# One softmax per pair of tiles in a fused attention and MLP kernel, and a bias joined by accumulating DMAs

## The chip, the cores and the metric

The kernel runs on one core of a Trainium2 chip. The metric is device time in microseconds (us), as the median of several executions. A core has a matrix engine (TensorE, "PE" in the profile, with its weight loads as "PEld"), a vector engine (VectorE, "DVE"), a scalar engine for activations (ScalarE, "ACT"), GpSimd ("POOL"), and SyncE ("SP"). In this kernel SP does nothing but issue DMAs. The engines run side by side and wait for one another by semaphores. In the traces of this case, SP's DMAs are issued in the order in which the program was written: in the changed kernel a load whose buffer VectorE had finished reading at 219.0 us was issued at 226.19 us, behind the two transposes written ahead of it (SP's lines are shown below).

An instruction that waits in SP's queue holds up every DMA written behind it.

## The reference, cut to what matters

```python
# S = 2048 positions, D = 576, H = 32 heads, W = 8 keys per position, spaced 2 apart
h  = x + softmax_w(q . k[s - 2w]) @ v[s - 2w] @ wo        # from layernorm(x) @ wqkv
h2 = h + gelu(layernorm(h) @ w1 + b1) @ w2 + b2           # F = 4608
```

Each position attends to itself and to the seven positions 2, 4, ..., 14 before it. The positions are cut into 16 tiles of 128, even tiles first, then odd ones, and eight *groups* (pairs of tiles) go through the rest of the kernel one after the other.

## The kernel before: the parts that matter

For every group, TensorE does three blocks: MLP1 (four "visits" of PSUM banks), the wo product of the next group, and MLP2. Beside it, VectorE and ScalarE prepare later groups: attention of the tiles e and f two groups ahead, and LayerNorm of the tiles c and d one group ahead.

Attention needs no matrix engine here. QK multiplies q by eight K rows and adds them up in a tree; PV does the same with V. Both use the one scratch tile `prod`. K and V of the eight tiles of one parity lie in a ring. After a tile has used a ring slot, the slot is refilled from DRAM with the rows shifted by one (`halo`), for the next tile of that parity:

```python
def halo(j, t):                       # t = 1: K, t = 2: V
    if j >= 2:
        ring = (None, k_ring, v_ring)[t]
        nc.sync.dma_start(out=ring[j % 2][:, j // 2, :], in_=kv_dram[j, 0:P, t - 1, :])

def pv_sum(j):
    att_pv_sum(j)                     # one 2.56 us multiply, three adds, on VectorE
    halo(j, 2)
```

So QK of f must wait until the K halo load issued after QK of e has landed, and PV of f waits for the V halo load issued after PV of e. LayerNorm's result crosses DRAM to be transposed:

```python
def ln2_send(j):                      # ScalarE, then two DMAs on SP's queue: hn -> td
    ...
    hn[j] = dma_out(y[:])
def ln2_in(j):                        # a transposing DMA on SP's queue: td -> hnT
    nc.sync.dma_start_transpose(out=hnT_slot(j), in_=hn.pop(j)[:])
def add_b2(j):                        # VectorE
    nc.vector.tensor_tensor(out=x_all[:, j, :], in0=h_of.pop(j)[:], in1=b2_bc[:], op=ALU.add)
def marker(mm_ins):                   # end of a half's visit, on GpSimd's queue
    nop = nc.gpsimd.nop().ins
    ...
```

The schedule of a group k, with c, d the next group and e, f the one after (cut):

```python
m1[0].append(c_(pv_t, d))                               # in MLP1: PV left over from the last group
m1[3] = [c_(att_qk, e)] + [c_(w2_sums, ...)]            # in MLP1, last visit: QK of e
ia[0] = [c_(exps, e), c_(wo_visit, (c, "B"), (d, "C")), c_(ln2_pair, c, d, e)]
ia[2] = [c_(pv_sum, e), c_(dma_tr_o, e)]                # in MLP2, first tile: PV of e
ib[0] = [c_(finish_out, g[0])]                          # evict the first tile of MLP2
ib[2] = [c_(att_qk, f)] + ([c_(halos, 7)] if k == 1 else [])   # in MLP2, second tile: QK of f
ib[32] = [c_(exps, f)]
```

In the trace of before, QK of e and QK of f start some 20 us apart (118.90 and 138.36 us in the second group), and PV of e and PV of f 16 us apart (132.53 and 148.65 us), with other work between.

## Time and profile before

| | before |
|---|---|
| time, median of runs | 371.8 us |
| TensorE / VectorE / ScalarE / GpSimd busy | 363.2 / 299.3 / 239.1 / 25.2 us |
| one group (MLP1 + wo + MLP2) | 17.79 + 2.21 + 17.75, period 37.74 us |
| TensorE waits over 0.3 us after 94 us | none |

First the busy times on the page of the kernel before (microseconds, share of the span, instructions):

```profile
PE 363.2 (98%) x4944; PEld 299.4 (81%) x4944; DVE 299.3 (81%) x452; ACT 239.1 (65%) x519; POOL 25.2 (7%) x35
```

A busy share does not yet say who sets the time. The chain of waits does. This is a part of it for the kernel before (start, length, what):

```profile
93.92 14.81 PE po L505 x120
108.72 17.79 PE pm L209 x324
126.52 2.21 PE pw L209 x36
128.72 17.75 PE po L505 x144
146.47 17.79 PE pm L209 x324
...
350.77 15.55 PE po L576 x126
366.35 0.46 DVE o_sb L599
```

Each line begins where the last one ended: from 93.9 us to the end the chain is TensorE and nothing else. VectorE is 81% busy and on the chain nowhere in that stretch, apart from the last eviction.

SP's queue in the kernel before, in the second group (start, length of issue; x2 is two in a row): hn of two tiles is written, transposed back, then the V halo load.

```profile
137.44 0.34 SPq L185 DMA_DIRECT2D td<-hn  x1
137.83 0.42 SPq L186 DMA_DIRECT2D td<-hn  x1
138.53 0.33 SPq L185 DMA_DIRECT2D td<-hn  x1
138.91 0.42 SPq L186 DMA_DIRECT2D td<-hn  x1
139.47 2.52 SPq L433 DMA_TRANSPOSE hnT<-td  x2
142.09 0.53 SPq L314 DMA_DIRECT2D kv_ring<-kv_dram  x1
```

And the DMA issues of the kernel before (count, KB each, median us from issue to landing):

```profile
td<-hn SPq DMA_DIRECT2D x14, 144.0 KB, 1.8
td<-hn SPq DMA_DIRECT2D x14, 16.0 KB, 1.6
hnT<-td SPq DMA_TRANSPOSE x14, 2.9
```

An hn write lands in 1.8 us, a transpose in 2.9 us.

### The profile page before, as it was taken

The numbers are of one execution on the slowest core, as the hardware profiler recorded it, in microseconds if no ns is written. First come the engines' busy times: TensorE is split into PE (matmuls) and PEld (weight loads), VectorE is DVE, ScalarE is ACT, GpSimd is POOL, SyncE is SP. The second block draws the span as 40 slices with busy tenths as digits, with TensorE's granted clock in tenths as the row PEclk, the third lists the DMA queues.
The fourth block names the chain that finished last, engine by engine and source line by source line (L and its number), as shares of the span: only waits on it lengthen the run. The fifth ranks groups of instructions, "written<-read, shape, count | busy, mean of one in ns | idle before, by whom it ended". The sixth has DMA issues, their size and how long they took to land.

```text
span 369.8 us, 11478 instructions
## 1 busy us (share of the span) xinstructions
PE 363.2 (98%) x4944; PEld 299.4 (81%) x4944; DVE 299.3 (81%) x452; ACT 239.1 (65%) x519; POOL 25.2 (7%) x35
## 2 busy tenths in 40 slices
PE   7999999999999999999999999999999999999996
PEld 4789877888788877887788778877887788778874
DVE  6899999999999798979897989889898986532332
ACT  2688756797738793679366936693669456735630
POOL 2322004000300010001000100000000000000000
PEclk9999999999999999999999999999999999999999
DMA  8979798956445104710431043104320411030000
GB/s 242 318 198 282 190 204 235 331 178 76 141 107 166 35 15 111 275 35 2 110 97 37 2 106 102 37 2 105 86 52 3 105 52 39 0 89 18 4 0 32
DMA packets 57265, 38.96 MB, mean 105 GB/s; under 512 B 31344, under 2 KB 55536, under 8 KB 57216
## 3 DMA queue, kind: packets, MB, share of 16 engines
q1 hardware_dynamic: 57056, 38.18, 38.6%
q8 instruction: 38, 0.62, 0.7%
q10 hardware_dynamic: 160, 0.07, 0.1%
q14 instruction: 11, 0.09, 0.1%
HBM read 19.92 MB, written 12.42 MB: 87 GB/s over the span
## 4 chain that ended last, share of the span: by engine, by line
PE 84%; DVE 11%; ACT 2%; POOL 1%; issue 1%; POOLq 0%; DVEq 0%
PE pm L209 37%; PE po L505 29%; PE po L576 8%; PE pw L209 5%; PE pq L209 4%; DVE ln_stats L145 2%; DVE prod L323 2%; DVE prod L362 1%; DVE prod L317 1%; PE busy L661 1%; DVE prod L366 1%; POOL ln_rstd L156 1%; ACT hT L490 1%; DVE ln_mv L146 1%; ACT L463 0%
## 5 line engine op out<-in xcount | busy, mean ns | idle before, releaser
L209 PE MATMUL pm<-hnT,w_sb 64*128 64x256 bf16 x2304 | 143.0, 269 | 0.5 <-ACT hT L490 0.5
L490 ACT ACTIVATE hT<-pm,b_sb 128x256 bf16<-128x256 f32 (+1 forms) x288 | 108.5, 498 | 48.4 <-PE pm L209 48.4
L209 PEld LDWEIGHTS <-w_sb 64*128 64x128 bf16 x2304 | 112.5, 94 | 15.0 <-issue 2.3
L505 PEld LDWEIGHTS <-hT 128*128 128x128 bf16 x864 | 84.0, 98 | 22.6 <-issue 1.7
L505 PE MATMUL po<-w2a_sb,hT 128*128 128x288 bf16 x672 | 84.5, 286 | 0.0
L209 PE MATMUL pq<-wq_sb,xnT 64*128 64x288 bf16 x768 | 54.0, 283 | 0.4 <-ACT xnT L255 0.2
L209 PEld LDWEIGHTS <-xnT 64*128 64x128 bf16 x864 | 44.1, 94 | 9.1 <-issue 0.4
L323 DVE TENSOR_TENSOR prod<-prod 128x2304 bf16<-128x2304 bf16 (+1 forms) x64 | 44.2, 691 | 2.1
L362 DVE TENSOR_TENSOR prod<-kv_ring,a 128x4608 bf16<-128x4608 bf16 x16 | 40.9, 2558 | 0.6
L317 DVE TENSOR_TENSOR prod<-kv_ring,q_all 128x4608 bf16<-128x4608 bf16 x16 | 40.8, 2552 | 0.2
L209 PE MATMUL pm<-hnT,w1h_sb 64*128 64x256 bf16 x288 | 39.4, 269 | 0.0
L366 DVE TENSOR_TENSOR prod<-prod 128x2304 bf16<-128x2304 bf16 (+1 forms) x32 | 33.9, 1058 | 1.1
L345 ACT ACTIVATE logits<-logits 128x256 f32<-128x256 f32 x16 | 6.7, 417 | 38.1 <-DVE logits L334 38.1
L423 POOL TENSOR_TENSOR ln_rstd<-ln_var,mhalf 128x1 f32<-128x1 f32 x14 | 11.3, 810 | 249.8 <-ACT ln_var L422 249.6
L505 PE MATMUL po<-w2b_sb,hT 128*128 128x288 bf16 x192 | 25.5, 286 | 0.0
L294 ACT CAST kv_ring<-pq 128x576 bf16<-128x576 f32 x32 | 19.4, 641 | 8.4 <-PE pq L209 8.4
L407 DVE TENSOR_TENSOR h<-pw,x_all 128x576 f32<-128x576 f32 x16 | 11.4, 751 | 14.0 <-PE pw L209 14.0
L209 PE MATMUL pw<-wo_sb,oT 64*128 64x288 bf16 x256 | 19.5, 283 | 0.2
L463 ACT ACT_TABLE_LOAD x14 | 18.0, 1283 | 0.2
L552 DVE TENSOR_TENSOR prod<-hT 128x512 f16<-128x512 f16 (+1 forms) x8 | 3.6, 455 | 17.6 <-ACT hT L490 17.6
L209 PEld LDWEIGHTS <-oT 64*128 64x128 bf16 x288 | 13.9, 94 | 4.3 <-POOLq L219 0.8
L345 ACT ACT_TABLE_LOAD x13 | 16.7, 1283 | 0.2
(98 smaller groups left out, 340.4 us busy)
## 6 DMA issues: line engine op xcount, KB each, us to landing
w_sb<-in_B_w_dram SPq DMA_DIRECT2D x6, 768.0 KB, 6.0
kv_ring<-kv_dram SPq DMA_DIRECT2D x28, 144.0 KB, 2.8
w2a_sb<-in_B_w_dram SPq DMA_DIRECT2D x4, 1008.0 KB, 6.5
kv_dram<-kv_ring SPq DMA_DIRECT2D x13, 288.0 KB, 3.5
out_dram<-o_sb SPq DMA_DIRECT2D x15, 144.0 KB, 2.9
td<-q_all SPq DMA_DIRECT2D x14, 144.0 KB, 2.4
td<-hn SPq DMA_DIRECT2D x14, 144.0 KB, 1.8
wq_sb<-in_A_wqkv_dram SPq DMA_DIRECT2D x3, 576.0 KB, 5.9
```

Source lines behind the costliest of these rows:

```text
L209: last = nc.tensor.matmul(duo["g"][r ^ swap][i], lhsT=lhsT, rhs=rhs, start=(swap == 0 and i == 0 and kt == 0), stop=(swap == 1 and kt == K ...
L294: pace[0] = nc.scalar.copy(out=dst.rearrange("p (d g h) -> p g d h", g=2, h=H // 2), in_=ps[:, :, 0:HALF].rearrange("p g (h d) -> p g d h" ...
L317: nc.vector.tensor_tensor(out=prod[:], in0=k_ring[j % 2], in1=q_all[:, j, :].unsqueeze(1) .to_broadcast([P, W, D]), op=ALU.mult)
L323: nc.vector.tensor_tensor(out=prod[:, :, o * H:o * H + n], in0=prod[:, :, a * H:a * H + n], in1=prod[:, :, c * H:c * H + n], op=ALU.add)
L345: nc.scalar.activation(out=logits[:], in_=logits[:], func=ACT.Exp, scale=SCALE)
L362: nc.vector.tensor_tensor(out=prod[:].rearrange("p w (d h) -> p w d h", h=H), in0=v_ring[j % 2].rearrange("p w (d h) -> p w d h", h=H), in ...
L366: nc.vector.tensor_tensor(out=prod[:, 0:n, :], in0=prod[:, 0:n, :], in1=prod[:, n:2 * n, :], op=ALU.add)
L407: nc.vector.tensor_tensor(out=h[:].rearrange("p (g c) -> p g c", g=2), in0=pw[:, :, 0:HALF], in1=x_all[:, j, :].rearrange("p (g c) -> p g ...
L463: nc.scalar.activation(out=warm[:], in_=mhalf[:], func=ACT.Gelu_apprx_tanh)
L490: pace[0] = nc.scalar.activation(out=hT[us[i // GF]][:, GF * r + i % GF, 0:N], in_=ps[:, r, i * N:(i + 1) * N], func=ACT.Gelu_apprx_tanh, ...
L505: nc.tensor.matmul(banks[half], lhsT=hT[f // (2 * GF)][:, f % (2 * GF), i * P:(i + 1) * P], rhs=w2_rows(f)[:, half * HALF:(half + 1) * HAL ...
L576: nc.tensor.matmul(bank, lhsT=l, rhs=r, start=(start and m == 0), stop=(m == NM - 1), skip_group_check=True)
```

## The change

Its intent is to relieve VectorE and ScalarE. One max, subtract, exp, sum, reciprocal and product per *pair* of tiles replaces one per tile, which also saves switching of ScalarE's tables between Exp and Gelu (28 table loads in the trace of before). For that, both QK stand together in MLP1 and both PV together in MLP2. The b2 adds leave VectorE: SP's queue copies b2 into `x_all`, and GpSimd's queue adds h to it with an accumulating DMA. The diff, cut to its core:

```diff
+    def put_b2(j):
+        nc.sync.dma_start(out=x_all[:, j, :], in_=b2_bc[:])
+
+    def accumulate_h(j):
+        nc.gpsimd.dma_start(out=x_all[:, j, :], in_=h_of.pop(j)[:], accum_op=ALU.add)
 ...
-        def ln2_pair(c, d, e, b2=True):
+        def ln2_pair(c, d):
             for j in (c, d):
                 ln2_h(j)
                 ln2_act(j)
             for j in (c, d):
-                if b2:
-                    add_b2(j)
+                put_b2(j)
+            for j in (c, d):
+                accumulate_h(j)
                 ln2_send(j)
             for j in (c, d):
                 ln2_in(j)
-            if e is not None:
-                att_den(e)
 ...
+                if k == 1:                       # changeover from the old order to the new
+                    m1[0].append(c_(pv_t, d))
+                    m1[1] = [c_(att_qk_a, e), c_(halo, e, 1), c_(att_qk_b, e, 0)]
+                    m1[3] = [c_(att_qk_a, f), c_(halo, f, 1)]
+                    ia[0] = wo + [c_(att_qk_b, f, 1), c_(att_max, (e, f)), c_(exps, e, f), c_(att_den, e, f)]
+                    ia[2] = [c_(pv_sum, e), c_(dma_tr_o, e), c_(halos, 4)]
+                elif e is not None:
+                    m1[1] = [c_(att_qk_pair, e, f)]
+                    m1[3] = [c_(w2_sums, *m) for m in T_SUMS.get(k, ())]
+                    ia[0] = [c_(exps, e, f)] + wo + [c_(att_den, e, f)]
+                    ia[2] = [c_(pv_sum, e), c_(dma_tr_o, e)]
 ...
-                    ib[2] = [c_(att_qk, f)] + ([c_(halos, 7)] if k == 1 else [])
-                    ib[32] = [c_(exps, f)]
+                    ib[2] = [c_(pv_sum, f), c_(dma_tr_o, f)] + ([c_(halos, 3)] if k == 1 else [])
```

The softmax tiles become four fixed tiles of double width, and the first LayerNorm's statistics move to another pool to make room.

More of the change, by code (lines that the diff above doesn't have):

```diff
@@ L82 @@
     prod = wpool.tile([P, W, D], BF16, name="prod")
+    logits = wpool.tile([P, 2, W, H], F32, name="logits")
+    probs = wpool.tile([P, 2, W, H], BF16, name="probs")
+    peak = wpool.tile([P, 2, H], F32, name="peak")
+    den = wpool.tile([P, 2, H], F32, name="den")
     qp_cm = tc.tile_pool(name="qkvw", bufs=1)
@@ L140, in ln_stats @@
         n = len(srcs)
-        stats = sb.tile([P, n, 2, nc.vector.BN_STATS_DIM], F32, tag=f"{tag}_stats", name=f"{tag}_stats", bufs=bufs)
-        mv = sb.tile([P, n, nc.vector.BN_AGGR_DIM], F32, tag=f"{tag}_mv", name=f"{tag}_mv", bufs=bufs)
+        pool = qp if tag.startswith("ln1") else sb
+        stats = pool.tile([P, n, 2, nc.vector.BN_STATS_DIM], F32, tag=f"{tag}_stats", name=f"{tag}_stats", bufs=bufs)
+        mv = pool.tile([P, n, nc.vector.BN_AGGR_DIM], F32, tag=f"{tag}_mv", name=f"{tag}_mv", bufs=bufs)
         for i, src in enumerate(srcs):
@@ L306, in tr_b1, with sides @@
         nc.scalar.copy(out=b1_sb[:], in_=pt)
-    e_of = {}
+    side = {}
+    def sides(js):
+        i = side[js[0]]
+        return slice(i, i + len(js))
     def halo(j, t):
@@ L324, in att_qk_add, with att_qk_b, att_max, att_qk_rest @@
                                     in1=prod[:, :, c * H:c * H + n], op=ALU.add)
-    def att_qk_b(j, skip=0):
+    def att_qk_b(j, i, skip=0):
+        side[j] = i
         att_qk_add(j, ((0, 0, 9), (0, 0, 4), (0, 0, 2), (0, 0, 1))[skip:])
-        logits = sb.tile([P, W, H], F32, tag="logits", name="logits", bufs=2)
-        nc.vector.tensor_tensor(out=logits[:], in0=prod[:, :, 0:H], in1=prod[:, :, 8 * H:9 * H], op=ALU.add)
+        nc.vector.tensor_tensor(out=logits[:, i], in0=prod[:, :, 0:H], in1=prod[:, :, 8 * H:9 * H], op=ALU.add)
         if j // 2 + 1 < W:
-            nc.vector.memset(logits[0:1, j // 2 + 1:W, :], -1e9)
-        mx = sb.tile([P, H], F32, tag="mx", name="mx")
-        nc.vector.tensor_reduce(out=mx[:], in_=logits[:].rearrange("p w h -> p h w"), axis=AX.X, op=ALU.max)
-        nc.vector.tensor_tensor(out=logits[:], in0=logits[:], in1=mx[:].unsqueeze(1).to_broadcast([P, W, H]),
-                                op=ALU.subtract)
-        e_of[j] = logits
-    def att_qk(j):
+            nc.vector.memset(logits[0:1, i, j // 2 + 1:W, :], -1e9)
+    def att_max(js):
+        n, sl = len(js), sides(js)
+        nc.vector.tensor_reduce(out=peak[:, sl], in_=logits[:, sl].rearrange("p i w h -> p i h w"), axis=AX.X, op=ALU.max)
+        nc.vector.tensor_tensor(out=logits[:, sl], in0=logits[:, sl],
+                                in1=peak[:, sl].unsqueeze(2).to_broadcast([P, n, W, H]), op=ALU.subtract)
+    def att_qk_rest(j, i, skip=0):
+        att_qk_b(j, i, skip)
+        att_max([j])
+    def att_qk(j, i):
         att_qk_a(j)
         halo(j, 1)
-        att_qk_b(j)
-    def att_exp(j):
-        logits = e_of[j]
-        nc.scalar.activation(out=logits[:], in_=logits[:], func=ACT.Exp, scale=SCALE)
+        att_qk_rest(j, i)
+    def att_qk_pair(e, f):
+        for i, j in enumerate((e, f)):
+            att_qk_a(j)
+            halo(j, 1)
+            att_qk_b(j, i)
+        att_max([e, f])
+    def att_exp(*js):
+        sl = sides(js)
+        nc.scalar.activation(out=logits[:, sl], in_=logits[:, sl], func=ACT.Exp, scale=SCALE)
     def att_pv(j):
@@ L349, in att_pv, with att_den @@
         att_pv_sum(j)
-    def att_den(j):
-        e = e_of.pop(j)
-        den = sb.tile([P, H], F32, tag="den", name="den")
-        nc.vector.tensor_reduce(out=den[:], in_=e[:].rearrange("p w h -> p h w"), axis=AX.X, op=ALU.add)
-        nc.vector.reciprocal(out=den[:], in_=den[:])
-        a = sb.tile([P, W, H], BF16, tag="a", name="a")
-        nc.vector.tensor_tensor(out=a[:], in0=e[:], in1=den[:].unsqueeze(1).to_broadcast([P, W, H]), op=ALU.mult)
-        e_of[j] = a
+    def att_den(*js):
+        n, sl = len(js), sides(js)
+        nc.vector.tensor_reduce(out=den[:, sl], in_=logits[:, sl].rearrange("p i w h -> p i h w"), axis=AX.X, op=ALU.add)
+        nc.vector.reciprocal(out=den[:, sl], in_=den[:, sl])
+        nc.vector.tensor_tensor(out=probs[:, sl], in0=logits[:, sl],
+                                in1=den[:, sl].unsqueeze(2).to_broadcast([P, n, W, H]), op=ALU.mult)
     def att_pv_sum(j):
-        a = e_of.pop(j)
+        a = probs[:, side.pop(j)]
         nc.vector.tensor_tensor(out=prod[:].rearrange("p w (d h) -> p w d h", h=H),
                                 in0=v_ring[j % 2].rearrange("p w (d h) -> p w d h", h=H),
-                                in1=a[:].unsqueeze(2).to_broadcast([P, W, Dh, H]), op=ALU.mult)
+                                in1=a.unsqueeze(2).to_broadcast([P, W, Dh, H]), op=ALU.mult)
         for n in (4, 2):
@@ L747 @@
             6: [c_(ln1_rstd, 10), c_(ln1_act, 8, 2), c_(halo, A[0], 1)],
-            7: [c_(att_qk_b, A[0]), c_(ln1_bias, 10), c_(ln1_act, 8, 3), c_(in_x, 0), c_(out_x, 1)],
-            8: [c_(att_qk_a, A[1]), c_(att_qk_b, A[1]), c_(ln1_act, 9, 0)],
+            7: [c_(att_qk_rest, A[0], 0), c_(ln1_bias, 10), c_(ln1_act, 8, 3), c_(in_x, 0), c_(out_x, 1)],
+            8: [c_(att_qk_a, A[1]), c_(att_qk_rest, A[1], 1), c_(ln1_act, 9, 0)],
             9: [c_(halo, A[1], 1), c_(in_x, 1)],
@@ L760 @@
             19: [c_(ln2, A[1])],
-            20: [c_(ln2_rstd, A[1]), c_(add_b2, A[1]), c_(ln2_bias, A[1]), c_(att_qk_b, A[2], 1)],
+            20: [c_(ln2_rstd, A[1]), c_(add_b2, A[1]), c_(ln2_bias, A[1]), c_(att_qk_rest, A[2], 0, 1)],
         }
@@ L817, in halos, with exps @@
                 store_halo(pending_halo.pop(0))
-        def exps(j):
-            att_exp(j)
+        def exps(*js):
+            att_exp(*js)
             gelu_table()
@@ L836 @@
             if k == 0:
-                m1[0] += [c_(halos, 1), c_(att_qk_a, d), c_(att_qk_b, d), c_(halo, d, 1)]
+                m1[0] += [c_(halos, 1), c_(att_qk_a, d), c_(att_qk_rest, d, 1), c_(halo, d, 1)]
                 mid[0] = [c_(exps, d)]
-                m1[1] = [c_(pv_t, c), c_(pv_t, d), c_(load_w2, 4), c_(att_qk, e)]
+                m1[1] = [c_(pv_t, c), c_(pv_t, d), c_(load_w2, 4), c_(att_qk, e, 0)]
                 ia[0] = [c_(wo_visit, (c, "B"))]
-                ia[12] = [c_(exps, e), c_(wo_visit, (d, "A")), c_(ln2_pair, c, d, e, False), c_(pv_sum, e), c_(dma_tr_o, e), c_(halos, 2)]
+                ia[12] = [c_(exps, e), c_(wo_visit, (d, "A")), c_(ln2_pair, c, d), c_(att_den, e), c_(pv_sum, e),
+                          c_(dma_tr_o, e), c_(halos, 2)]
@@ L842 @@
                 ib[0] = [c_(finish_out, g[0])]
-                ib[4] = [c_(att_qk, f)]
+                ib[4] = [c_(att_qk, f, 1)]
                 ib[32] = [c_(exps, f)]
             elif c is not None:
-                m1[0].append(c_(pv_t, d))
+                wo = [c_(wo_visit, (c, "B"), (d, "C")), c_(ln2_pair, c, d)]
                 if k == 1:
-                    m1[0] += [c_(add_b2, j) for j in g]
-                if e is not None:
-                    m1[3] = m1.get(3, []) + [c_(att_qk, e)] + [c_(w2_sums, *m) for m in T_SUMS.get(k, ())]
-                    ia[0] = [c_(exps, e)]
@@ L852 @@
-                ia[0] = ia.get(0, []) + [c_(wo_visit, (c, "B"), (d, "C")), c_(ln2_pair, c, d, e)]
+                    m1[0].append(c_(pv_t, d))
[8 more added lines that the diff above has]
+                    ia[2] = [c_(pv_sum, e), c_(dma_tr_o, e)]
+                else:
+                    ia[0] = wo
@@ L853 @@
                 ib[0] = [c_(finish_out, g[0])]
                 if e is not None:
-                    ia[2] = [c_(pv_sum, e), c_(dma_tr_o, e)]
-                    ib[2] = [c_(att_qk, f)] + ([c_(halos, 7)] if k == 1 else [])
-                    ib[32] = [c_(exps, f)]
+                    ib[2] = [c_(pv_sum, f), c_(dma_tr_o, f)] + ([c_(halos, 3)] if k == 1 else [])
             if g in fast:
```

## The prediction

> **What bounds the kernel now.** TensorE. The page gives it 98% busy at full granted clock. The chain of waits, in order of time, is TensorE alone from 93.9 us to the last eviction at 366.4: per group of two tiles 17.79 us MLP1, 2.21 us wo, 17.75 us MLP2, with no gap (period 37.74). The change touches no matmul. VectorE (81%) and ScalarE (65%) are off the chain there. The gaps before 79 us lie in code the change leaves alone. So the change can remove nothing from the chain; it can only add waits.
>
> **What it removes, per full group.** VectorE: two b2 adds (0.75 each) and some fixed cost of the small softmax operations (max 0.59, subtract 0.42, sum 0.59, reciprocal 0.35, product 0.42 become one double-width operation per pair): about 2 us of about 34. ScalarE: one pair of table loads (2 x 1.28) and an exp: about 2.8 us. I value both at zero.
>
> **What it adds.** Two b2 copies on SP's queue and two accumulating GpSimd-queue DMAs per group, and 4 us or more of PV moved from MLP1 into MLP2. GpSimd's queue also carries the no-ops that mark ends of a visit; accumulations issue just after wo, about 10 us before the next marker, so I expect no wait there. The Trainium skill, "DMA: Bandwidth & Descriptors", section "SWDGE vs HWDGE vs iDMA", says accumulation is tied to GpSimd's software descriptor path; the before trace has no such DMA to compare. Two cost estimates from the durations above: pair max 1.1, pair softmax finish 2.5 us.
>
> **Where I expect new waits: in the changeover groups, k=1 and k=2; later groups fit (about 32 us of VectorE in 37.7).**
> 1. k=1 does a leftover PV, a QK, half a QK, then after wo the other half, exp, and both PVs. VectorE estimate: exp ready 138, softmax 140.7, PV e 145.9, eviction 146.6, PV f 151.9, and only then the second tile's eviction, 152.6. The second group of MLP1's second visit wants that PSUM pair at 151.5: about 1 us of TensorE wait (0 to 2.5).
> 2. SP's queue is in order: transpose of PV f waits for its write (2 to 3.3 us as in before), three K/V stores follow (0.7 each), so the first odd halo load issues only near 161 and lands near 164 (2.8 us median). VectorE's second QK of k=2 waits for it; the pair's max, the weight sums and then h after wo come near 175 instead of 166.0. LayerNorm and transposes take about 12 us more (before: h 166.0, last transpose issued 179.7), so hnT lands near 187 where MLP1 wants it at 185.4: about 2 us (0 to 4.5).
> 3. At the end of k=0, hnT lands about 0.3 us before it is needed; accumulation traffic could cost up to 1 us.
>
> Sum about 2.7 us.
>
> **Prediction: 374.5 us; range 371.6 to 378.5.** Faster by over 2%: 0.01; within 2%: 0.92; slower by over 2%: 0.07.
>
> **What would show it.** Right: TensorE matmul busy total unchanged; chain still TensorE, but with a VectorE eviction of MLP2's second tile near 150 us and a DMA or ScalarE piece near 185 us; VectorE idle waiting for a halo load near 160 us; ScalarE with about five table-load pairs fewer; steady groups still 37.74 us apart. Wrong: chain unbroken (time equal), or waits of TensorE on GpSimd's queue at every MLP1.
>
> **What would make it wrong.** Descriptor work for the accumulations slow enough under VectorE's traffic to block markers (several us per group, over 2% slower); accumulations delaying the hnT transposes in every group; the halo stores draining faster than I estimate (then no loss); a hidden cost of before that VectorE's relief cures, which I see no sign of.

## The result, and the profile after

The first four runs of the changed kernel gave a median of 388.56 us (383.81 to 394.67), against 371.79 (371.74 to 371.90) of the kernel before. That is 4% slower and outside the predicted range. Two of the four runs were slow: they were over 1.5% above the fastest of their own kernel; this kernel scatters by itself. Ratios here are the mean time of one kernel's fast runs over the mean of the other's fast runs of the same rounds, so not quite the ratio of the medians: 1.037 (95% interval 1.032 to 1.042) from those runs, and 1.044 (1.037 to 1.051) from a later repetition.

The busy times of the changed kernel:

```profile
PE 365.5 (95%) x4944; PEld 310.3 (80%) x4944; DVE 285.6 (74%) x413; ACT 224.8 (58%) x499; POOL 40.0 (10%) x49
```

The intent was met: VectorE does 13.7 us less and ScalarE 14.3 us less. None of it became time. The span went from 369.8 to 385.6 us. The waits list of the changed kernel (who waited for whom, us in total, times, longest) shows new entries for TensorE and VectorE:

```profile
PE pm L214 <- DVE o_sb L657: 6.8, 4, 1.9
PE pm L214 <- DMA hnT<-td: 4.6, 2, 2.3
PE pm L214 <- DVE logits L345: 1.7, 1, 1.7
DVE prod L381 <- DMA kv_ring<-kv_dram: 25.3, 4, 6.4
DVE prod L326 <- DMA kv_ring<-kv_dram: 10.0, 6, 4.0
DVE rest L624 <- DMA x_all<-h: 4.4, 1, 4.4
```

The first three are the loss: 13.1 us of TensorE waiting in MLP1 blocks. (The third, at 110.31 us, is put down to VectorE's `logits`, which merely came last by the profile; b2_only below has the same wait at the same place, put down to hnT.) Adding 1.7 us of half clock (below) gives 14.8 of the 15.8 us. The fourth and fifth lines are where they come from. L381 is the PV multiply, L326 the QK multiply. VectorE waits four times for about 6.3 us until a V halo load has landed, before PV of f. The chain of waits of the changed kernel, from one such wait to the next (many short pieces left out), is a closed loop that hardly touches TensorE:

```profile
186.75 2.40 DMA kv_ring<-kv_dram
189.25 2.57 DVE prod L381
...
194.40 0.75 DVE o_sb L657
195.15 2.48 DVE prod L326
...
199.73 2.36 DMA kv_ring<-kv_dram
202.11 2.57 DVE prod L326
...
212.85 1.34 DVE h L426 x2
...
221.07 3.77 DMA td<-hn
224.89 1.20 SPq L452
226.19 2.46 DMA kv_ring<-kv_dram
228.75 2.57 DVE prod L381
```

Read it as follows. The V halo load lands, so PV of f runs, then the eviction of MLP2's second tile (`o_sb`, for which TensorE waits), then QK of e, a K halo load, QK of f, the weight sums, and h of the next group. LayerNorm, the hn write and the transposes follow, and only then comes the next V halo load, because it stands behind all of that *in SP's queue*. From PV of f to PV of f this takes 228.75 - 189.25 = 39.5 us, and the following turns take about as long. TensorE needs 37.74 us per group, so the loop now sets the pace, with a wait of 1.5 to 1.9 us each time: these waits end at 195.20, 234.70, 274.14 and 313.95 us, which is 39.5, 39.4 and 39.8 us apart. The load needs nothing from LayerNorm. SP's queue in that stretch of the changed kernel shows it (it answers to the lines of before):

```profile
219.17 0.35 SPq L190 DMA_DIRECT2D td<-hn  x1
...
220.69 0.33 SPq L190 DMA_DIRECT2D td<-hn  x1
221.07 0.46 SPq L191 DMA_DIRECT2D td<-hn  x1
221.69 4.40 SPq L452 DMA_TRANSPOSE hnT<-td  x2
226.19 0.52 SPq L323 DMA_DIRECT2D kv_ring<-kv_dram  x1
```

The same order as before, so the order of these instructions is not new. What is new is that VectorE now wants the load at once (PV of f follows PV of e directly), and that the two transposes take 4.40 us to get issued instead of 2.52. They wait for the hn writes. The DMA issues of the changed kernel say why:

```profile
td<-hn SPq DMA_DIRECT2D x14, 144.0 KB, 2.2
x_all<-h POOLq DMA_DIRECT2D x14, 144.0 KB, 4.4
td<-hn SPq DMA_DIRECT2D x14, 16.0 KB, 3.7
```

The second, small part of an hn write lands after 3.7 us instead of 1.6. The accumulations (4.4 us each to landing) are in flight at just that time.

The last wait has a second part. The stretches of the changed kernel around the start of the last MLP1 (busy time and count per engine, then granted clock, DMA share, GB/s):

```profile
346.00:348.00 2.00, 1.21 (x12) 1.03 (x14) 0.00 (x0) 0.00 (x0) 0.00 (x0) 0.68 0.50 149
348.00:350.00 2.00, 2.00 (x24) 1.63 (x20) 0.00 (x0) 0.00 (x0) 0.00 (x0) 0.50 0.00 0
350.00:352.00 2.00, 2.00 (x38) 1.94 (x36) 0.00 (x0) 0.33 (x1) 0.00 (x0) 0.97 0.00 0
```

After TensorE had waited 2.25 us for hnT, it worked at half clock for 3.3 us, until about 350.1 us; this MLP1 took 19.47 us instead of 17.79.

So the theory, called S below: the pairing closes a loop through the order of SP's queue, and the accumulations stretch it. Its rival, A: the accumulations alone do the damage, wherever hn has to travel. A second rival: the accumulations are innocent.

### The profile page after: what moved, and what is told of

Same layout as the page of the kernel before. It is cut to its first block, busy times and chain, and to the rows that moved or that the text cites. A ratio compares the mean times of both kernels' runs of the same rounds, so it can differ in the third digit from the quotient of the medians.

```text
span 385.6 us, 11482 instructions
## 1 busy us (share of the span) xinstructions
PE 365.5 (95%) x4944; PEld 310.3 (80%) x4944; DVE 285.6 (74%) x413; ACT 224.8 (58%) x499; POOL 40.0 (10%) x49
## 3 DMA queue, kind: packets, MB, share of 16 engines
q0 software_dynamic: 2016, 2.07, 5.2%
## 4 chain that ended last, share of the span: by engine, by line
DVE 38%; PE 33%; DMA 13%; ACT 6%; issue 3%; SPq 3%; POOL 2%; ACTq 0%; DVEq 0%; POOLq 0%
PE pm L214 18%; PE po L601 7%; DVE prod L332 7%; DVE prod L326 7%; DVE prod L381 6%; DMA kv_ring<-kv_dram 5%; PE po L530 5%; DVE prod L385 4%; DMA td<-hn 4%; DVE ln_stats L150 2%; DVE peak L344 2%; POOL ln_rstd L442 2%; SPq L452 1%; DMA x_all<-in_A_x_dram 1%; PE pw L214 1%
## 5 line engine op out<-in xcount | busy, mean ns | idle before, releaser
L214 PE MATMUL pm<-hnT,w_sb 64*128 64x256 bf16 x2304 | 144.9, 271 | 13.5 <-DVE o_sb L657 6.8
L214 PEld LDWEIGHTS <-w_sb 64*128 64x128 bf16 x2304 | 121.5, 95 | 21.5 <-issue 13.1
L381 DVE TENSOR_TENSOR prod<-kv_ring,probs 128x4608 bf16<-128x4608 bf16 x16 | 40.9, 2558 | 25.7 <-DMA kv_ring<-kv_dram 25.3
L326 DVE TENSOR_TENSOR prod<-kv_ring,q_all 128x4608 bf16<-128x4608 bf16 x16 | 40.9, 2553 | 10.0 <-DMA kv_ring<-kv_dram 10.0
L214 PE MATMUL pm<-hnT,w1h_sb 64*128 64x256 bf16 x288 | 41.1, 272 | 0.0
L442 POOL TENSOR_TENSOR ln_rstd<-ln_var,mhalf 128x1 f32<-128x1 f32 x14 | 13.7, 979 | 248.4 <-ACT ln_var L441 248.4
L161 POOL TENSOR_TENSOR ln_rstd<-ln_veps,mhalf 128x1 f32<-128x1 f32 (+2 forms) x13 | 13.2, 1016 | 49.0 <-DVE ln_veps L155 42.6
L214 PEld LDWEIGHTS <-oT 64*128 64x128 bf16 x288 | 15.3, 94 | 2.9 <-POOLq L224 0.8
L214 PEld LDWEIGHTS <-w1h_sb 64*128 64x128 bf16 x288 | 15.6, 95 | 0.8
L150 DVE BATCH_NORM_STATS2 ln_stats<-x_all 128x6 f32<-128x288 bf16 x32 | 12.8, 443 | 2.0 <-DMA x_all<-in_A_x_dram 2.0
```

Of the source, the lines that this page charges most:

```text
L150: nc.vector.bn_stats(out=stats[:, i, c, :], in_=src[:, c * HALF:(c + 1) * HALF])
L161: nc.gpsimd.tensor_tensor(out=rstd[:], in0=veps[:], in1=mhalf[:].to_broadcast([P, n]), op=ALU.pow)
L214: last = nc.tensor.matmul(duo["g"][r ^ swap][i], lhsT=lhsT, rhs=rhs, start=(swap == 0 and i == 0 and kt == 0), stop=(swap == 1 and kt == K ...
L326: nc.vector.tensor_tensor(out=prod[:], in0=k_ring[j % 2], in1=q_all[:, j, :].unsqueeze(1) .to_broadcast([P, W, D]), op=ALU.mult)
L381: nc.vector.tensor_tensor(out=prod[:].rearrange("p w (d h) -> p w d h", h=H), in0=v_ring[j % 2].rearrange("p w (d h) -> p w d h", h=H), in ...
L442: nc.gpsimd.tensor_tensor(out=rstd[:], in0=var[:], in1=mhalf[:], op=ALU.pow)
```

## The experiments

Every run was made beside runs of the kernel before on the same chip (medians 371.46, 371.53 and 371.75 us in the three batches). All outputs were correct except where a wrong result is announced.

| run | what | median us | ratio to before (95%) |
|---|---|---|---|
| b2_only | only the DMA half of the change | 374.56 | 1.009 (1.007 to 1.012) |
| pair_only | only the softmax half | 375.85 | 1.015 (1.010 to 1.020) |
| early_halo | changed, V halo load of e early | 380.67 | 1.022 (1.017 to 1.027) |
| pair_fixed | pair_only, both reorderings of SP | 372.13 | 1.002 (1.000 to 1.003) |
| stores_moved | changed, K/V stores late | 386.63 | 1.041 (1.037 to 1.045) |
| both_moved | changed, both reorderings of SP | 375.90 | 1.015 (1.009 to 1.021) |
| b2_copy | b2_only, no accumulation (wrong result) | 373.74 | 1.006 (1.004 to 1.007) |
| all_fixed | both_moved, accumulations later | 372.73 | 1.003 (1.001 to 1.005) |
| late_acc | changed, accumulations later | 377.00 | 1.014 (1.013 to 1.016) |
| pair_dummy | pair_only plus idle DMA traffic | 382.50 | 1.029 (1.026 to 1.032) |
| b2_nocast | b2_only, no cast, no accumulation (wrong result) | 372.00 | 1.001 (1.000 to 1.003) |
| after_again | changed, repeated | 387.81 | 1.044 (1.037 to 1.051) |

### The two halves alone

b2_only is the kernel before with this edit (the b2 adds left over in the second group's MLP1 go too):

```diff
             for j in (c, d):
-                if b2:
-                    add_b2(j)
+                put_b2(j)
+            for j in (c, d):
+                accumulate_h(j)
                 ln2_send(j)
```

> The kernel before, with only the b2 half of the change (two b2 copies on SP's queue and two accumulating DMAs on GpSimd's queue per pair). Theory S (the order of SP's queue costs most, the accumulations only add two single delays): first MLP1 after the accumulations late by about 1.7 us as in the changed kernel (110.3 instead of 108.7 us), the last MLP1 late by 2.2 us plus some 1.7 us at half clock, steady groups 37.74 us apart: 376 to 378 us. Rival A (the accumulations slow every group's hnT transposes and are the main cause): steady groups over 39 us apart, 382 us or more.

Measured: 374.56 us, 3.1 more than before. Steady groups are 37.74 us apart. The first MLP1 after accumulations starts at 110.50 us (before: 108.72), the last one about 0.9 us late and at full clock, so the time came out below the 376 expected. Rival A falls: in a schedule with slack the accumulations cost two single waits (1.91 and 0.85 us).

pair_only is the changed kernel with the adds back on VectorE:

```diff
             for j in (c, d):
-                put_b2(j)
-            for j in (c, d):
-                accumulate_h(j)
+                if (c, d) != tuple(GROUPS[1]):   # those are added in the next MLP1, as in before
+                    add_b2(j)
                 ln2_send(j)
```

> The changed kernel with the b2 adds back on VectorE: the softmax half alone. The loop PV f, QK e, QK f, weight sums, h, LayerNorm, transposes, halo load, PV f took 39.5 us in the changed kernel; without accumulations the hn write to DRAM should take 1.8 us as in before instead of 3.7, so the loop should be about 37.7 and just keep pace. Theory S: one late hnT near 186 us of about 2 us, perhaps one late eviction, VectorE still waiting 4 us or more for the halo load before PV f: 374 to 378 us. Rival A: within 1 us of before (371 to 373). Rival S-only (accumulations innocent): 382 us or more.

Measured: 375.85 us, 4.4 more. The second rival (accumulations innocent) falls as well. The waits list of pair_only:

```profile
DVE prod L381 <- DMA kv_ring<-kv_dram: 14.0, 4, 4.9
PE pm L214 <- DVE o_sb L657: 3.5, 3, 1.7
```

One part of the expectation was too good: the loop was to take 37.7 us and just keep pace. TensorE's waits for the eviction ended at 191.09, 229.77 and 268.71 us, 38.7 and 38.9 us apart, so the loop is still about 1 us too long; the waits were 1.7, 0.8 and 1.0 us. The late hnT expected near 186 us did not come. The waits for the eviction are there without a single accumulation; only smaller.

3.1 and 4.4 make 7.5 us, and together the halves cost 16 to 17. The rest is their meeting, which the later runs take apart.

### The order of SP's queue

early_halo changes the order of emission so that the V halo load of e stands ahead of the hn writes. Within VectorE's queue and within ScalarE's queue nothing moves:

```diff
                 accumulate_h(j)
-                ln2_send(j)
+                if e is None:
+                    ln2_send(j)
+            if e is not None:
+                att_den(e, f)
+                pv_sum(e)
+                for j in (c, d):
+                    ln2_send(j)
             for j in (c, d):
                 ln2_in(j)
```

> The changed kernel with one change of order on SP's queue: from the third group on, the V halo load of tile e is issued before the two hn writes and hnT transposes instead of behind them; VectorE's and ScalarE's own orders stay. Theory S: VectorE's 6.3 us wait before PV f gone, the evictions no longer late (6.8 us of TensorE waits gone), groups from the third on 37.74 us apart; the waits at 110, 188 and 346 us stay: 378 to 382 us. Rival A: still over 39 us per group, 384 us or more.

Measured: 380.67 us, within the range and for the reason given, but not entirely. (Single runs scatter from 377.39 to 386.33 us, the longest at clock 0.987.) The waits list of early_halo has no wait of PV (L381) for a load any more and no wait of TensorE for an eviction. The wait has partly moved to the next link of the loop, QK of f waiting for the K halo load of e, which stands in SP's queue behind two more DMA transposes:

```profile
DVE prod L326 <- DMA kv_ring<-kv_dram: 22.4, 6, 6.5
PE pm L214 <- DMA hnT<-td: 9.2, 5, 3.0
```

So groups were not all back at 37.74 us, as I had expected: hnT was late five times.

stores_moved takes the second group's bulk K/V stores out of the way instead:

```diff
-                    ia[2] = [c_(pv_sum, e), c_(dma_tr_o, e), c_(halos, 4)]
+                    ia[2] = [c_(pv_sum, e), c_(dma_tr_o, e), c_(halos, 2)]
...
-                    m1[3] = [c_(w2_sums, *m) for m in T_SUMS.get(k, ())]
+                    m1[3] = [c_(halos, 5 if k == 2 else 0)] + [c_(w2_sums, *m) for m in T_SUMS.get(k, ())]
...
-                    ib[2] = [c_(pv_sum, f), c_(dma_tr_o, f)] + ([c_(halos, 3)] if k == 1 else [])
+                    ib[2] = [c_(pv_sum, f), c_(dma_tr_o, f)]
```

> The changed kernel with one change: five of the seven K/V stores of the second group go behind the third group's two halo loads on SP's queue. Theory S: the first QK wait (4.0 us at 158.8) shrinks to 2 us or less, hnT of the fourth group no longer late (2.3 us gone), but the loop through SP's queue still takes about 39.4 us per group and TensorE is caught by it a group later: 382 to 388 us, a little below the changed kernel. If the stores were the whole cause: 377 or less.

Measured: 386.63 us. The QK wait it aims at fell from 4.00 to 1.72 us and the late hnT from 2.31 to 0.36, and yet nearly nothing was won. The waits for evictions after it came to 7.4 us (changed kernel: 6.8): what is gained at the entrance of a loop that is too slow is lost again at its next link.

pair_fixed puts both reorderings on pair_only; both_moved puts both on the changed kernel.

> The softmax half alone (b2 on VectorE), the V halo load of e issued early, and five of the seven K/V stores of the second group moved behind the third group's halo loads. Theory S: every wait of TensorE after 94 us gone, 371.5 to 372.5 us, the same as before, VectorE and ScalarE busier by nothing and still no gain, since TensorE was the bound. If a wait of another kind (GpSimd markers, the double-width softmax itself) mattered: over 374.

> The changed kernel with both reorderings of SP's queue (V halo load of e early, five K/V stores late), b2 still by accumulating DMAs right after wo. Theory S: what is left is what the accumulations cost by themselves, 1.7 us at 110, about 2 us and perhaps half-clock time before the last MLP1, and 0 to 3 us where hnT is late in between because the hn writes take 3.7 us: 375 to 379 us.

pair_fixed: 372.13 us, and its chain is again TensorE alone, with the old lengths and no gap from 94.87 us on:

```profile
94.87 14.81 PE po L530 x120
109.67 17.79 PE pm L214 x324
127.47 2.21 PE pw L214 x36
129.67 17.75 PE po L530 x144
```

The whole softmax half, with its two PV in MLP2 and its double-width operations, thus costs nothing once the loads are placed well. The 0.95 us by which this profile lies behind is already there before 94 us (its waits list has TensorE waiting 0.7 us there for the load of the QKV weights); the quickest of its runs, 371.45 us, equals before. both_moved: 375.90 us, as expected; 3.8 us more than pair_fixed, which differs from it only in how b2 is added. In its profile, a quick run of 374.66 us, TensorE waits 2.4 us for a late hnT, 1.8 of them at the first MLP1; the longest of its runs took 379.79 us.

### What in the accumulations costs

b2_copy and b2_nocast change one line of b2_only each. Their outputs are wrong, which doesn't matter for the times.

```diff
-        nc.gpsimd.dma_start(out=x_all[:, j, :], in_=h_of.pop(j)[:], accum_op=ALU.add)
+        nc.gpsimd.dma_start(out=x_all[:, j, :], in_=h_of.pop(j)[:])      # b2_copy: f32 -> bf16
+        nc.gpsimd.dma_start(out=x_all[:, j, :], in_=b2_bc[:])            # b2_nocast: bf16 -> bf16
```

> The kernel b2_only with the accumulation taken out of the two GpSimd-queue DMAs: they copy and cast the same h to the same place (result wrong on purpose: b2 is missing from the output). It tells which property slows the hn writes beside them (3.6 us against 1.8). If it is the accumulation (read and add at the destination): hn writes back near 2 us, the DMA lands in about 2 to 3 us instead of 4.5, TensorE not late at 110 us, 371.5 to 372.5. If it is the cast or the software queue: all as in b2_only, 374 to 375.

> The kernel b2_only with the two GpSimd-queue DMAs turned into plain bf16 copies of b2 to the same place (wrong on purpose), no cast and no accumulation. b2_copy, which casts, gave hn writes of 2.8 us and 373.7. If the cast or its wider reads matter: hn writes near 2 us, 371.5 to 372.5. If any transfer from GpSimd's queue at that moment delays them: as b2_copy, 373 to 374.

| | 144 KB DMA lands after | small hn write lands after | share of the DMA engines | packets | time |
|---|---|---|---|---|---|
| no such DMA (before) | | 1.6 us | | | 371.8 us |
| plain copy (b2_nocast) | 2.5 us | 2.5 us | 1.5% | 672 | 372.0 us |
| with cast (b2_copy) | 3.3 us | 3.3 us | 3.4% | 2016 | 373.7 us |
| cast and accumulation (b2_only) | 4.5 us | 3.8 us | 5.0% | 2016 | 374.6 us |

(The hn write meant is the 16 KB part; share and packets are of GpSimd's DMA queue in each profile.) Neither expectation was met cleanly, and the truth is a staircase: the plain copy costs next to nothing, the cast most of it, the accumulation some more (0.3, 2.2 and 3.1 us over the kernel before of the same batch). The three write the same bytes. The time that the transfers hold the DMA engines goes up with each step, and the hn writes beside them land later with each step. This does not separate the cast from its source, which is twice as wide.

### The halves meeting

late_acc keeps the changed kernel's order of loads on SP. It moves twelve accumulations to the fourth visit of the next MLP1, where no hn is under way, and it takes out the other two: the last pair's b2 is added on VectorE.

```diff
             for j in (c, d):
-                put_b2(j)
+                add_b2(j) if c in fast[-1] else put_b2(j)      # last pair: VectorE (an if/else in the run)
             for j in (c, d):
-                accumulate_h(j)
                 ln2_send(j)
...
+            if 0 < k < len(GROUPS) - 1:
+                m1[3] = [c_(accumulate_h, j) for j in g] + m1.get(3, [])
```

> The changed kernel, SP's order as the change has it, but the accumulations issued a group later (fourth visit of MLP1, away from the hn writes) and the last pair's b2 on VectorE. It tells whether the two halves interact through the hn writes. Theory (the accumulations stretch the hn writes from 1.8 to 3.7 us, and that stretches the loop through SP's queue past the 37.74 us that TensorE needs): hn writes 1.8 us, and the time falls to that of pair_only, 375 to 378 us, though all 12 remaining accumulations still run. Rival (they cost wherever they stand): 382 us or more.

Measured: 377.00 us, almost pair_only's time, although 12 accumulations still run and still take 3.8 us each. Not all of the gain comes from moving them: the last MLP1 is on time in this profile (2.25 us late in the changed kernel), and there the two accumulations are gone altogether. The waits for evictions, 3.2 us in place of 6.8, belong to the ones that were moved. The DMA issues of late_acc:

```profile
td<-hn SPq DMA_DIRECT2D x14, 144.0 KB, 1.8
x_all<-h POOLq DMA_DIRECT2D x12, 144.0 KB, 3.8
td<-hn SPq DMA_DIRECT2D x14, 16.0 KB, 1.6
```

pair_dummy is the test in the other direction: pair_only, where nothing accumulates, with useless copies of h to DRAM issued from GpSimd's queue right after wo.

```diff
+                spare = dram.tile([P, D], BF16, tag="spare", name="spare", bufs=2)
+                nc.gpsimd.dma_start(out=spare[:], in_=h_of[j][:])
                 if (c, d) != tuple(GROUPS[1]):
                     add_b2(j)
```

> The kernel pair_only with traffic added and nothing accumulated: right after wo GpSimd's queue copies each h (cast to bf16) into an unused DRAM tile, 14 in all; b2 stays on VectorE. The same theory the other way round: hn writes 2.5 us or more, the loop over 38.5 us, 379 to 385 us instead of 375.9. If only the accumulating kind matters, or the wait of the output on it: 376 to 377.

Measured: 382.50 us, 6.7 us more than pair_only (6.4 if each is taken against the kernel before of its own batch), from copies that nobody reads. The copies landed after 3.3 us, and both parts of the hn write after 2.8 us (pair_only: 1.8 and 1.6):

```profile
td<-hn SPq DMA_DIRECT2D x14, 144.0 KB, 2.8
spare<-h POOLq DMA_DIRECT2D x14, 144.0 KB, 3.3
td<-hn SPq DMA_DIRECT2D x14, 16.0 KB, 2.8
```

The same kind of traffic, though into SBUF and not DRAM, cost b2_copy 2.2 us in the schedule with slack. The interaction is shown in both directions: traffic beside the hn writes costs little where hn has slack, and costs every group where hn's path has become part of the loop.

### A version with both halves

all_fixed is both_moved with late_acc's edit.

> Both halves of the change with their costs moved: both reorderings of SP's queue, the accumulations issued a group later (in the fourth visit of MLP1, when no hn write or transpose is in flight), the last pair's b2 on VectorE. Theory S: no wait of TensorE after 94 us, hn writes 1.8 us, 371.4 to 372.6 us, same as before and not better, as TensorE is the bound. If accumulating DMAs cost by their mere presence (GpSimd's queue, port): over 374.

Measured: 372.73 us, 0.1 above the range. Hn writes are at 1.8 us, and TensorE waits once after 94 us for more than 0.3 us, where none was expected: 0.8 us until 152.22 us, for the eviction behind PV of f in the changeover group. It is not better than before, as theory S says: the chain was TensorE's to begin with. No version beat the kernel before, and the runs point to none.

### The scatter

> The changed kernel unaltered, for its scatter beside these runs: 383 to 395 us as before, with granted clocks of 0.987 to 1.0; runs with the lower clock the longer ones if half-clock stretches after TensorE's waits are part of the scatter. Where the clock falls to half, it should follow a wait of TensorE of about 2 us or more.

Measured: 384.52 to 389.78 us with clocks of 0.991 to 1.0. The run at clock 1.0 took 386.11 us, so the loss does not need the half clock; the longest of the first runs, 394.67 us, had 0.987. In two traces the clock fell to about half, after TensorE waits of 2.25 us (changed kernel) and 1.94 us (stores_moved). In early_halo's profile a wait of 3.00 us left it at full, and in the changed kernel's own trace so did one of 2.31 us. The length of the wait alone does not decide it in these traces; what does was not tested.

The profile of after_again: TensorE's waits in MLP1 come to 13.0 us (13.1 in the first profile), 7.2 of them for evictions, 1.7 at the first MLP1 and 2.6 for hnT in the changeover. The last hnT is only 0.36 us late there, but two others are late by 0.6 us each. So the loop, the changeover and the first wait repeat; the expensive end does not.

## Why the prediction was wrong

**Right.** TensorE alone was the bound; the removed 13.7 and 14.3 us of VectorE and ScalarE work were worth zero, and ScalarE lost five pairs of table loads (28 loads to 18). The markers on GpSimd's queue were not held up: TensorE's waits on that queue are 0.8 us in total, as in before. Step 2 (the changeover) was right in mechanism and size: the first odd K halo load was predicted to be issued near 161 and to land near 164 us, h near 175, hnT near 187, TensorE 2 us late; measured were 159.8 and 162.7, 173.4, 188.2 and 2.3 us.

**The step that failed: "later groups fit (about 32 us of VectorE in 37.7)".** This compares a sum of work with a period. The work does fit: VectorE is 74% busy. But the order does not fit. I had traced SP's queue for the changeover group and then, for the steady groups, only added up VectorE's durations. The V halo load of e stands in SP's queue behind the LayerNorm of the next group, so VectorE's two PV, back to back in the new schedule, have all of that between them: 6.3 us of waiting per group, a loop of 39.5 us, and 6.8 us of TensorE waits for late evictions. The groups that were to stay 37.74 us apart came 39.4 to 39.8 us apart. In pair_only the loop without accumulations still takes 38.7 us.

**Step 3 was right in kind and too small.** I gave the accumulations' traffic up to 1 us at the end of the first group; it took 1.7. The accumulations land after 4.4 us, where the plain 144 KB copies of b2 on SP's queue take 2.0, and b2_nocast and b2_copy show that a shorter transfer there delays hn less. What I named as a way to be wrong, "accumulations delaying the hnT transposes in every group", happened: the late hn writes make the loop longer, though in the old schedule the same delay is harmless (b2_only).

**Step 1** (an eviction about 1 us late in the changeover group) did not show in the changed kernel. The eviction started at 152.22 us, close to the 152.6 predicted, but the first group's 1.7 us delay had also put off TensorE's need for it. With that delay gone it appears in all_fixed (0.8 us) and late_acc (0.4 us), but not in pair_only or pair_fixed, which add b2 on VectorE; there VectorE waits 0.8 us for the exp instead of 2.0. Why was not tested.

**Not foreseen**: the last MLP1. The second-last group's final sums reuse the buffers of h and so wait 4.4 us for an accumulation to land; its hnT is also late, by 2.25 us. With the half clock that followed, this end cost about 4 us in the profiled run. In the profile of after_again the same end cost 0.4 us, so its size is not steady.

The predicted sum had 2.7 us of waits. The trace has 13.1, of which 6.8 are the steady loop, 2.3 the changeover, 1.7 and 2.3 the first and last hnT, and 1.7 us of half clock come on top.

## What to carry to other kernels

Before two uses of one buffer are moved next to each other, look up what refills the buffer between them, and read that DMA's place in its issuing queue: everything written ahead of it in that queue now lies on the path. For a steady loop, trace one dependency all the way around (engine, queue, DMA, back) and compare that length with the bound engine's period; a sum of busy times per engine cannot show it. And when work of an engine that is not the bound is swapped for DMAs, ask which small, urgent transfers will be in flight at that moment: here the change cost 1.2 us instead of 16 once the loads stood early in their queue, the accumulations were issued where nothing waited beside them, and the last pair's b2 was back on VectorE.

## What the Trainium skill lacked or had wrong

- "DMA: Bandwidth & Descriptors", section "SWDGE vs HWDGE vs iDMA", ties accumulation and cast to GpSimd's software path (used in the prediction), but gives no cost for them. Its fit for that path in the section "Anatomy of one DMA — SWDGE (gpsimd) path", 2.0 us plus bytes over 436 GB/s, makes an estimate of 2.3 us for 144 KB. The plain copy agrees (2.5 us in b2_nocast); with a cast it was 3.3 us, with cast and accumulation 4.4 to 4.5 us, and the DMA counted 144 packets instead of 48.
- The same page, section "Issuing engines are not separate DMA queues", says that DMAs of all issuing engines run on the same 16 DMA engines and interleave. The runs are consistent with it and give it a size: two casting or accumulating 144 KB transfers made a 16 KB write beside them land after 3.3 to 3.8 us instead of 1.6.
- "TensorE: Matmul & The Clock Gate", section "Why this matters for your kernels", advises no idle gaps above about 3 us between matmul bursts. Here the clock fell to half after waits of 2.25 us and 1.94 us, both shorter than that, and stayed full after one of 3.00 us. The section "What's actually happening" gives the throttled state after at least one idle window of about 3.4 us, which is also longer than the two waits; no run here isolates what decided. The half-clock stretch of about 3.4 us, worked out from the granted clock in both traces, agrees with the length of that window.
- The pages describe where a DMA waits for its semaphores, but none was found to draw the consequence that, in a closed loop, an in-order DMA issue queue couples unrelated paths: here a 2.4 us load that needed nothing from LayerNorm waited behind it, 6.3 us of VectorE's time per group.
